# Batch 1's q and k transposed on TensorE instead of by DMA, the second weight's loads issued behind the first's, and batch 1's norms moved behind batch 0

## The chip, the cores and the metric

The kernel runs on one core of a Trainium2 chip. The metric is the device time of one execution in microseconds (us). The engines are named as in the profile: PE is TensorE's matrix multiply, PEld its weight load, DVE is VectorE, ACT ScalarE, POOL GpSimd and SP SyncE, which here only issues DMAs. The kernel's order is written by hand: an engine's instructions stand in its queue in that order, and one whose operand is not ready holds up those behind it.

## The reference

An attention with normed q and k is followed by a mixer block with a low-rank token mix:

```python
def _attn_ref(q, k, v, g_q, g_k):          # q, k, v: (8, 12, 448, 64)
    q_n, k_n = rmsnorm(q, g_q), rmsnorm(k, g_k)      # over the head's 64 values
    scores = matmul(q_n, k_n.T) / sqrt(64)
    attn = softmax(scores)
    return matmul(attn, v)

def _moe_ref(x, U, V, w_ch1, w_ch2):       # x: (8, 448, 768), heads side by side
    xt = x.transpose(0, 2, 1)
    h = xt @ U @ V                          # rank 32
    u = x + h.transpose(0, 2, 1)
    ch = maximum(u @ w_ch1, 0) @ w_ch2      # 768 -> 3072 -> 768
    return u + ch
```

Inputs and output are float32; the kernel multiplies in bf16. There are 8 batches of 448 rows, and the two weights are 9.4 MB each in float32, 4.7 MB each once they stand in SBUF as bf16.

## The kernel before

**Units.** A pair `p` is two heads of one batch; a batch has six pairs, so batch 0 has pairs 0 to 5 and batch 1 pairs 6 to 11. Loads go by triples of the form `t = p // 2`, four heads each: `load(t)` issues four 256 KB transfers on SP (q and k for the pairs 2t and 2t+1), `load_v(t)` one of 512 KB for v. Two buffers `qkL` take q and k in turn (a third lies in `hT` while that is unused), so `load(5)` needs the buffer of `load(3)`, which is read by `scale(6)` and `scale(7)`.

**The path of one pair.** `squares(p)` (POOL, L199) squares q and k; `reduce(p)` (DVE, L205) sums over 64 values into the PSUM bank `rs_bank`; `rsqrt(p, n)` (ACT, L209 and L210) takes the inverse root for n pairs at once; `scale(p)` (DVE, L218) writes normed q and k in bf16 to `qkn`. Two buffers take the squares, so `squares(p)` needs `reduce(p - 2)` done. Then q and k must be turned so that the 64 values lie on partitions (`qkT`). There are two ways:

- `transposes(p)`: eight 112x112 transposes on PE (L240) into one PSUM tile `pt`, then on DVE a multiplication of q by the gains (L242) and a copy of k (L246).
- `dma_transposes(p)`: one transposing DMA on SP (L249), SBUF to SBUF; the gains follow as `gains(p)` on ACT, in place (L254).

Batch 0 takes the first way, all later batches the second. `scores(p, kcs)` (PE, L263) then multiplies, `expo(p, kc)` (ACT, L268) exponentiates, `values(p, hh)` (PE, L284) multiplies by v, and DVE divides (L287, L288, L291). `cast_v(t)` on POOL (L188) turns v into bf16.

**The mixer.** `mix_t`, `mix_u` and `mix_x` do the low-rank mix on PE, with results taken out by DVE or ACT; `turn_u` transposes u by DMA into `uA` or `uB`. `mlp(b)` is a generator: 24 pieces of six matmuls `ph` (L364), each followed by a relu into `hT` (all on ACT for batch 0), then the second layer in pieces of six matmuls `po` (L384), `osb` on DVE (L388) and the stores on SP. PSUM tiles `ph`, `po`, `o`, `px`, `pm`, `pt` share three buffers of `ps_mm`.

**The order** is written by hand. Batch 0's attention runs first, pair by pair, in `pair(p)`. `begin` does the matmuls of the first four `ph` pieces into idle score buffers. Then, for each batch b, `weave` runs the fill `mlp(b)` between the items of `attention(b + 1)` and `mixing(b + 1)`: an item's weight sets how many columns of the fill are run before it, as a share of a total (for batch 0, 0.70 of the fill's 18,432 columns over the attention and 0.12 over the mixing; what is left runs at the end). `attention(1)` works ahead: at pair p it scales and transposes pair p + 2, and at pairs 7, 9 and 11 reduces the pairs of two triples later. It also issues `squares(10)` and `squares(11)` at pair 6, although both have been issued ahead of it.

**Weights.** `load_w1(i)` and `load_w2(half, i)` are cast during the DMA and are issued by POOL, six of each. The six of the first weight are issued within `pair(0)` to `pair(2)`, between casts and squares; those of the second stand behind all of batch 0.

Of the kernel before, what the change touches and what calls it, by code (L numbers as in the profile page):

```python
# [17 lines left out]
def kernel(  # L18
# [29 lines left out]
    NT, NP = B * 3, B * 6  # L48
# [46 lines left out]
    def rs_of(p, n=1):  # L95

        c = 16 * (p % 6)
        return rs_bank[:, c:c + 16 * n]
# [62 lines left out]
    def load_w2(half, i):  # L161
        hs, c = slice(half * HALF, (half + 1) * HALF), slice(8 * i, 8 * (i + 1))
        nc.gpsimd.dma_start(w2b[:, half, c], w2r[:, c, hs])
# [19 lines left out]
    def load_v(t):  # L183
        rows, src = heads(v, HG * t, HG)
        nc.sync.dma_start(v_of[t][0:rows], src)

    def cast_v(t):
        nc.gpsimd.tensor_copy(vas[t % NV][:, :, :, 0:D], v_of[t][0:SP].rearrange("p h (j d) -> p h j d", d=D))  # L188

    def squares(p, eng="pool", parts=(slice(0, 1024),)):  # L190
        t, a = divmod(p, 2)
        src = qk_of[t][0:SP, a].rearrange("p s h c -> p (s h c)")
        if p not in sqs:
            sqs[p] = norm.tile([SP, 2 * 2 * NJ * D], FP32, tag="sq", name="sq")
        for c in parts:
            if eng == "act":
                nc.scalar.activation(sqs[p][:, c], src[:, c], AF.Square)
            else:
                nc.gpsimd.tensor_tensor(sqs[p][:, c], src[:, c], src[:, c], OP.mult)  # L199

    def reduce(p, parts=(slice(0, 16),)):
        rs = rs_of(p)
        sq = sqs[p].rearrange("p (g d) -> p g d", d=D)
        for c in parts:
            nc.vector.tensor_reduce(rs[:, c], sq[:, c], AX, OP.add)  # L205

    def rsqrt(p, n=1):
        rs = rs_of(p, n)
        nc.scalar.activation(rs, rs, AF.Ln, bias=eps)  # L209
        nc.scalar.activation(rs, rs, AF.Exp, scale=-0.5)  # L210
# [37 lines left out]
    def dma_transposes(p):  # L248
        nc.sync.dma_start_transpose(out=qkTs[p % NQ][:, 0:SQK].rearrange("p (m r) -> p m r", r=SP),  # L249
                                    in_=qkns.pop(p).rearrange("p j g d -> p (j g d)"))  # L250

    def gains(p):
        qT = blocks(p)[:, :, 0]
        nc.scalar.activation(qT, qT, AF.Copy, scale=gg)  # L254
# [142 lines left out]
    def attention(b):  # L397
        items = []

        def add(weight, fn, *args):  # L400
            items.append((weight, lambda: fn(*args)))

        for p in range(b * 6, b * 6 + 6):
            t, odd = divmod(p, 2)
            add(1, scores, p, (0, 1))
            add(0, expo, p, 0)
            if p + 2 < NP:
                add(0, scale, p + 2)
                add(0, dma_transposes, p + 2)
            add(1, expo, p, 1)  # L410
            if p % 6:
                add(1, values, p - 1, 0)
            if t + 2 < NT:
                for a in range(2):
                    if odd:
                        add(0, reduce, 2 * t + 4 + a)
                    else:
                        add(0, squares, 2 * t + 4 + a)
            add(1, scores, p, (2, 3))
            add(0, expo, p, 2)  # L420
            if p % 6:
                add(1, values, p - 1, 1)
            if odd and t + 2 < NT:
                add(0, rsqrt, 2 * t + 4, 2)
            if odd and t + 3 < NT:
                add(0, load, t + 3)
                add(0, load_v, t + 3)
            if not odd and t + 1 < NT:
                add(0, cast_v, t + 1)
            if p + 1 < NP:  # L430
                add(0, gains, p + 1)
            add(1, expo, p, 3)
        add(1, values, b * 6 + 5, 0)
        add(1, values, b * 6 + 5, 1)
        return items

    def weave(fill, total, items):
        weights = sum(w for w, _ in items)
        done = due = 0.0
        for w, piece in items:  # L440
            due += w * total / max(weights, 1)
            while done < due:
                n = next(fill, None)
                if n is None:
                    break
                done += n
            piece()
# [22 lines left out]
    def pair(p):  # L470


        scores(p, (1,))
        expo(p, 0)
        if p == 0:
            scale(1)
        elif 1 < p < 5:
            rsqrt(p + 2)
        if 0 < p < 5:
            transposes(p + 1)  # L480
        if p >= 2:
            mix_t(0, [slice((p - 2) * P, (p - 1) * P)])
        if p:
            values(p - 1, 0)

        scores(p, (2,))
        expo(p, 1)
        if p == 0:
            transposes(1)
            reduce(2)  # L490
        elif p < 5:
            if p == 1:
                rsqrt(3)
            scale(p + 2)
        if p == 4:
            dma_transposes(6)
        if p:
            values(p - 1, 1)
        if p == 0:
            load(3)  # L500
            load_w1(0)
            cast_v(0)
            load_w1(1)
            squares(4)
            setup_late()
            load_w1(2)
        if p == 1:
            cast_v(1)
            setup_U()
            load_v(3)  # L510
            load_w1(3)
        if p == 2:
            load_w1(4)
            cast_v(2)
            load_w1(5)
            load(4)
            load_v(4)

        if 0 < p < 5:
            reduce(p + 3)  # L520
            squares(p + 5)
        scores(p, (3,))
        expo(p, 2)

        if p < 5:
            scores(p + 1, (0,))
        expo(p, 3)
        if p == 0:
            rsqrt(2)
            scale(2)  # L530
            reduce(3)
            squares(5)
        if p >= 2:
            mix_u(p - 2)

    with tc.manual_schedule():
        halves = (slice(0, 512), slice(512, 1024))
        groups = (slice(0, 8), slice(8, 16))
        load_pair(nc.sync, 0, 0, 0)
        load_pair(nc.scalar, 0, 1, 0)  # L540
        nc.scalar.preload_act_table_set("natural_log_exp_and_others")
        load_pair(nc.sync, 0, 0, 1)
        load_pair(nc.sync, 0, 1, 1)
        load_g()
        load(1)
        load_v(0)
        load_mix()
        load(2)
        load_v(1)
        load_v(2)  # L550
        setup()
        heat(NWARM)
        squares(0, "act", halves)
        squares(1, "act", halves)
        reduce(0, groups)
        rsqrt(0)
        scale(0, (slice(0, 2), slice(2, 4)))
        nc.gpsimd.tensor_mul(gg, gg, gk2)
        transposes(0)
        reduce(1)  # L560
        rsqrt(1)
        squares(2)
        squares(3)
        scores(0, (0,))
        for p in range(6):
            pair(p)
        mix_t(0, [slice(4 * P, 5 * P)])
        values(5, 0)
        mix_u(4)
        values(5, 1)  # L570
        begin(range(2), range(5))
        mix_t(0, [slice(5 * P, 6 * P)])
        begin(range(2, 4), range(5))
        mix_u(5)
        begin(range(4), (5,))
        gains(6)
        rsqrt(7)
        scale(7)
        dma_transposes(7)
        reduce(8)  # L580
        squares(10)
        cast_v(3)
        for half in range(2):
            for i in range(3):
                load_w2(half, i)
        for b in range(B):
            fill = mlp(b)
            if b == 0:
                for _ in range(4):
                    next(fill)  # L590
                load(5)
                load_v(5)
                reduce(9)
                squares(11)
                rsqrt(8, 2)
                extra = [(0, lambda i=i, h=h: mix_x(0, i, h)) for i in range(3) for h in range(2)]
                items = attention(1)
                step = len(items) // 7
                for n, x in enumerate(extra):
                    items.insert((n + 1) * step + n, x)  # L600
                weave(fill, volume(0) * 0.70, items)
                weave(fill, volume(0) * 0.12, mixing(1))
            elif b + 1 < B:
                weave(fill, volume(b % 2) * 0.72, attention(b + 1))
                weave(fill, volume(b % 2) * 0.12, mixing(b + 1))
            for _ in fill:
                pass
# [30 lines left out]
```

## Time and profile before

| | before |
|---|---|
| three runs, us | 630.65, 632.24, 633.34 (median 632.24) |
| the profiled execution's own time, us | 632.71 |
| its span, first to last instruction, us | 630.7 |
| PE busy | 592.5 us, 94% of the span |
| DVE, ACT, POOL busy | 305.7, 257.6, 130.0 us |
| mean granted TensorE clock | 0.962 of full speed |
| bytes moved by DMA | 73.63 MB |

The span's 40 slices are 15.8 us each; a digit is the busy share in tenths, and PEclk is the clock granted to TensorE:

```profile
PE   5876788999999999999999999999999999999996
POOL 6544711402023032022022033022023000000000
PEclk8668978999999999999999999999999999999999
DMA  8997999564425444464325444454425410050011
```

PE is below nine tenths in the first seven slices (110 us) and in the last. The clock is below full in the same stretch, and the 16 DMA engines are close to fully busy there; from about slice 8 on the picture repeats with a period of two batches, which is why batches 2 and 3 can serve as a measure for batches 0 and 1.

### The profile page before, as it was taken

What the parts mean: (1) busy time and instruction counts of PE and PEld (TensorE: products, weight loads), DVE (VectorE), ACT (ScalarE), POOL (GpSimd) and SP (SyncE); (2) the same over time, 40 slices, a digit from 0 to 9 for tenths busy, and PEclk for the clock granted to TensorE, in tenths of its full rate; (3) what the DMA queues carried; (4) which work ended last, traced back from release to release, by engine and by line L of the source; (5) the groups of instructions that cost most, each with busy time, mean ns of one, the idle gap of its engine ahead of it and who ended that gap; (6) DMA issues with size and microseconds to landing.
All of it is one profiled execution on the core that took longest, in us unless ns stands there. A gap on an engine that the chain in (4) does not pass through costs nothing.

```text
span 630.7 us, 11153 instructions
## 1 busy us (share of the span) xinstructions
PE 592.5 (94%) x4637; PEld 321.7 (51%) x4658; DVE 305.7 (48%) x614; ACT 257.6 (41%) x410; POOL 130.0 (21%) x111
## 2 busy tenths in 40 slices
PE   5876788999999999999999999999999999999996
PEld 2553344544455555554455555554455555554563
DVE  4853334655545366645545366645545364432211
ACT  5752564416551267316551267316551167202100
POOL 6544711402023032022022033022023000000000
PEclk8668978999999999999999999999999999999999
DMA  8997999564425444464325444454425410050011
GB/s 244 238 245 123 190 225 222 154 139 116 102 58 158 96 130 130 116 132 124 102 58 154 98 132 130 119 127 125 88 73 144 98 33 16 27 101 1 0 51 50
DMA packets 113746, 73.63 MB, mean 117 GB/s; under 512 B 62384, under 2 KB 110112, under 8 KB 113696
## 3 DMA queue, kind: packets, MB, share of 16 engines
q1 hardware_dynamic: 102160, 63.22, 40.8%
q0 software_dynamic: 10944, 9.44, 9.7%
q8 instruction: 36, 0.59, 0.4%
q10 hardware_dynamic: 592, 0.26, 0.2%
q14 instruction: 14, 0.11, 0.1%
HBM read 56.78 MB, written 11.01 MB: 107 GB/s over the span
## 4 chain that ended last, share of the span: by engine, by line
PE 75%; DMA 13%; DVE 7%; ACT 2%; issue 1%; POOL 0%; SPq 0%; DVEq 0%; ACTq 0%; POOLq 0%
PE po L384 33%; PE ph L364 29%; DMA qkT<-qkn 9%; PE sc L263 6%; PE o L284 5%; DVE rs_bank L205 4%; DMA qk<-in_k_dram 4%; PE px L334 1%; ACT E L268 1%; PE pm L313 1%; DVE hT L369 1%; ACT hT L367 1%; DMA uB<-x 1%; DVE x L288 1%; ACT qkT L254 0%
## 5 line engine op out<-in xcount | busy, mean ns | idle before, releaser
L384 PE MATMUL po<-w2b,hT 128*128 128x384 bf16 x1344 | 239.7, 328 | 1.3 <-DVE osb L388 1.3
L268 ACT ACTIVATE E<-sc 112x896 bf16<-112x896 f32 x192 | 170.4, 916 | 76.2 <-PE sc L263 75.9
L384 PEld LDWEIGHTS <-hT 128*128 128x128 bf16 x1344 | 126.7, 98 | 90.8 <-issue 13.4
L364 PEld LDWEIGHTS <-w1b 128*128 128x128 bf16 x1128 | 104.6, 99 | 118.3 <-issue 28.5
L199 POOL TENSOR_TENSOR sq<-qk 112x1024 f32<-112x1024 f32 x46 | 86.7, 1892 | 348.4 <-DMA qk<-in_k_dram 291.5
L367 ACT ACTIVATE hT<-ph 128x384 bf16<-128x384 f32 (+1 forms) x104 | 56.2, 541 | 214.8 <-PE ph L364 214.8
L364 PE MATMUL ph<-uB,w1b 128*128 128x512 bf16 x555 | 131.5, 379 | 3.1 <-DMA uB<-x 1.1
L364 PE MATMUL ph<-uA,w1b 128*128 128x384 bf16 x552 | 105.1, 337 | 5.6 <-DVE xs L291 5.2
L369 DVE TENSOR_SCALAR hT<-ph 128x512 bf16<-128x512 f32 (+1 forms) x84 | 53.2, 633 | 80.3 <-PE ph L364 80.0
L284 PEld LDWEIGHTS <-E 112*128 112x128 bf16 x1536 | 64.7, 101 | 20.3 <-DVE qkT L246 3.6
L284 PE MATMUL o<-va,E 112*128 112x65 bf16 x1536 | 69.2, 199 | 4.4 <-DVE qkT L246 3.4
L263 PE MATMUL sc<-qkT 64*128 64x448 bf16 x376 | 58.4, 373 | 11.1 <-ACT hT L367 5.3
L205 DVE TENSOR_REDUCE rs_bank<-sq 112x16 f32<-112x1024 f32 (+1 forms) x49 | 58.9, 1201 | 17.5 <-POOL sq L199 9.4
L388 DVE TENSOR_TENSOR osb<-po,x 128x384 f32<-128x384 f32 x48 | 26.8, 558 | 73.7 <-PE po L384 73.5
L218 DVE TENSOR_TENSOR qkn<-qk,rs_bank 112x1024 bf16<-112x1024 f32 (+1 forms) x47 | 55.9, 1191 | 11.0 <-ACT rs_bank L210 10.7
L287 DVE RECIPROCAL rec<-o 128x4 f32<-128x4 f32 x96 | 17.4, 181 | 88.4 <-PE o L284 88.3
L263 PEld LDWEIGHTS <-qkT 64*128 64x128 bf16 (+1 forms) x384 | 14.1, 97 | 49.7 <-issue 37.9
L288 DVE TENSOR_TENSOR x<-o,rec 128x192 bf16<-128x192 f32 x96 | 34.3, 358 | 3.3
L336 DVE TENSOR_TENSOR x<-px,x 128x384 bf16<-128x384 f32 x48 | 25.9, 554 | 18.9 <-PE px L334 18.8
L254 ACT ACTIVATE qkT<-qkT,gg 128x448 bf16<-128x448 bf16 x42 | 27.8, 662 | 9.5 <-DMA qkT<-qkn 9.5
L188 POOL CAST va<-vt 112x1024 bf16<-112x1024 f32 x23 | 23.8, 1039 | 1.7 <-DMA vt<-in_v_dram 1.7
L291 DVE TENSOR_TENSOR xs<-o,rec 64x64 bf16<-64x64 f32 x96 | 20.8, 217 | 0.7
(60 smaller groups left out, 140.4 us busy)
## 6 DMA issues: line engine op xcount, KB each, us to landing
qk<-in_q_dram SPq DMA_DIRECT2D x45, 256.0 KB, 4.3
qk<-in_k_dram SPq DMA_DIRECT2D x44, 256.0 KB, 4.6
vt<-in_v_dram SPq DMA_DIRECT2D x22, 512.0 KB, 6.0
w1b<-in_moe_w_ch_dram POOLq DMA_DIRECT2D x6, 768.0 KB, 15.1
w2b<-in_moe_w_ch_dram POOLq DMA_DIRECT2D x6, 768.0 KB, 26.8
out_dram<-osb SPq DMA_DIRECT2D x8, 336.0 KB, 2.8
out_dram<-osb SPq DMA_DIRECT2D x8, 288.0 KB, 2.8
out_dram<-osb SPq DMA_DIRECT2D x8, 240.0 KB, 2.7
```

The lines of the kernel that those rows point to most:

```text
L199: nc.gpsimd.tensor_tensor(sqs[p][:, c], src[:, c], src[:, c], OP.mult)
L205: nc.vector.tensor_reduce(rs[:, c], sq[:, c], AX, OP.add)
L218: nc.vector.tensor_tensor(qkns[p][:, :, c].rearrange("p j g d -> p g j d"), qk_of[t][0:SP, a].rearrange("p s h (j d) -> p (s h) j d", d=D) ...
L254: nc.scalar.activation(qT, qT, AF.Copy, scale=gg)
L263: nc.tensor.matmul(sc[0:n, hh, 0:S], flat[pp, c:c + n], blocks(p)[pp, :, 0], start=True, stop=True)
L268: nc.scalar.activation(Es[p % NE][:, :, PAD + kc * S:PAD + (kc + 1) * S], scs.pop((p, kc))[0:SP, :, 0:S], AF.Exp, scale=float(D) ** 0.5)
L284: nc.tensor.matmul(o[:, i, :], E[:, hh, c:c + P], va[:, hl, kc, :], start=(kc == 0), stop=(kc == NJ - 1))
L288: nc.vector.tensor_tensor(x3[:, :, d0:d0 + D], o[:, t0:t0 + 3, 0:D], rec[:, t0:t0 + 3].rearrange("p c -> p c ()").to_broadcast([P, 3, D]), ...
L364: nc.tensor.matmul(ph, w1b[:, dc, hc * P:(hc + 1) * P], u[:, dc, :], start=(dc == 0), stop=(dc == KD - 1))
L367: nc.scalar.activation(hT[:, hc, 0:n], ph, AF.Relu)
L369: nc.vector.tensor_relu(hT[:, hc, 0:n], ph)
L384: nc.tensor.matmul(po, hT[:, hc, i * P:(i + 1) * P], w2b[:, half, hc], start=(hc == 0), stop=(hc == KH - 1))
```

## The change

It has three parts. Batch 1's pairs 6 to 11 go the way of `transposes` (PE and DVE) instead of `dma_transposes` and `gains`; `attention(1)` issues `transposes(p + 1)` at pair p with weight 0.5. The six `load_w2` are issued in `pair(2)`, behind `load_w1(5)`. The norms of pairs 6 to 9 (squares, reduce, rsqrt, scale) leave `pair(1)` to `pair(4)` and stand behind batch 0 and `begin`, apart from `squares(6)` and `squares(7)`, which come in `pair(4)`. The second issue of `squares(10)` and `squares(11)` is gone. Eight pieces of the fill instead of four run ahead of `attention(1)`, and the shares of the weave go from 0.70 to 0.62 and from 0.12 to 0.08.

```diff
@@ attention(b)
             if p + 2 < NP:
                 add(0, scale, p + 2)
-                add(0, dma_transposes, p + 2)
+                if p >= 10:
+                    add(0, dma_transposes, p + 2)
...
                     if odd:
                         add(0, reduce, 2 * t + 4 + a)
-                    else:
+                    elif p > 6:
                         add(0, squares, 2 * t + 4 + a)
...
-            if p + 1 < NP:
+            if p < 11:
+                add(0.5, transposes, p + 1)
+            elif p + 1 < NP:
                 add(0, gains, p + 1)
@@ pair(p)
-        elif 1 < p < 5:
+        elif 1 < p < 4:
             rsqrt(p + 2)
...
-        elif p < 5:
+        elif p < 4:
             if p == 1:
                 rsqrt(3)
             scale(p + 2)
-        if p == 4:
-            dma_transposes(6)
...
             load_w1(5)
             load(4)
             load_v(4)
-
-        if 0 < p < 5:
+            for half in range(2):
+                for i in range(3):
+                    load_w2(half, i)
+
+        if 0 < p < 3:
             reduce(p + 3)
-            squares(p + 5)
+        if p == 4:
+            squares(6)
+            squares(7)
@@ after begin
-        gains(6)
-        rsqrt(7)
+        cast_v(3)
+        reduce(6)
+        squares(8)
+        reduce(7)
+        squares(9)
+        rsqrt(6, 2)
+        scale(6)
         scale(7)
-        dma_transposes(7)
-        reduce(8)
-        squares(10)
-        cast_v(3)
-        for half in range(2):
-            for i in range(3):
-                load_w2(half, i)
         for b in range(B):
             fill = mlp(b)
             if b == 0:
...
                 load(5)
                 load_v(5)
+                reduce(8)
+                squares(10)
                 reduce(9)
                 squares(11)
+                for _ in range(2):
+                    next(fill)
+                transposes(6)
+                for _ in range(2):
+                    next(fill)
                 rsqrt(8, 2)
...
-                weave(fill, volume(0) * 0.70, items)
-                weave(fill, volume(0) * 0.12, mixing(1))
+                weave(fill, volume(0) * 0.62, items)
+                weave(fill, volume(0) * 0.08, mixing(1))
```

## The prediction

> **What bounds the kernel now.** I read the stages first, cutting the span where the matmuls of a new batch begin (46.9 is `begin`, then mlp(1), mlp(2), ...). Columns: stage, its length, then PE, PEld, DVE, ACT, POOL busy (instructions), granted clock, DMA share, GB/s.
>
> ```profile
> 33.70:46.90 13.20, 9.82 (x111) 6.49 (x112) 7.95 (x23) 7.74 (x12) 5.95 (x5) 0.62 1.18 246
> 46.90:138.30 91.40, 74.46 (x565) 39.58 (x564) 40.55 (x78) 36.71 (x66) 32.76 (x23) 0.89 0.96 176
> 138.30:217.40 79.10, 78.52 (x594) 40.59 (x599) 38.40 (x77) 32.09 (x50) 14.26 (x9) 1.00 0.42 105
> 217.40:280.40 63.00, 62.16 (x539) 35.83 (x539) 37.23 (x76) 29.85 (x48) 14.22 (x9) 1.00 0.53 129
> 280.40:359.50 79.10, 78.53 (x594) 40.60 (x599) 39.66 (x78) 32.09 (x50) 14.26 (x9) 1.00 0.40 106
> ```
>
> From 138.3 on PE is busy all the time at full clock: it bounds, and the change touches nothing there. mlp(2) with attention(3) takes 63.0 us; the like work of mlp(0) with attention(1) takes 91.4. That stage, and the 13 us ahead of it, hold what can be had. Next the waits of PE in it (engine, line, what it waited for: us, times, longest):
>
> ```profile
> PE sc L263 <- ACT hT L367: 5.3, 2, 5.1
> PE ph L364 <- DVE xs L291: 5.2, 1, 5.2
> PE sc L263 <- ACT qkT L254: 2.4, 2, 2.2
> PE ph L364 <- DMA uB<-x: 1.1, 1, 1.1
> ```
>
> And the timeline at the three longest idle times, from 33.7 on:
>
> ```profile
> 33.23 1.88 POOL L199 TENSOR_TENSOR sq<-qk 112x1024 f32<-112x1024 f32 x1 [6.94 <-DMA qk<-in_k_dram]
> 35.15 1.23 DVE L205 TENSOR_REDUCE rs_bank<-sq 112x16 f32<-112x1024 f32 x1 [3.16 <-POOL sq L199]
> 36.28 0.44 DVE L242 TENSOR_SCALAR qkT<-pt,gg 128x448 bf16<-128x448 bf16 x1
> 37.08 1.06 PE L284 MATMUL o<-va,E 112*128 112x65 bf16 x16 [3.38 <-DVE qkT L246]
> ...
> 39.68 20.52 SPq L249 DMA_TRANSPOSE qkT<-qkn  x2
> 56.66 0.67 ACT L254 ACTIVATE qkT<-qkT,gg 128x448 bf16<-128x448 bf16 x1 [5.14 <-DMA qkT<-qkn]
> 58.49 0.56 PE L263 MATMUL sc<-qkT 64*128 64x448 bf16 x2 [5.13 <-ACT hT L367]
> ...
> 62.24 0.38 SPq L176 DMA_DIRECT2D qk<-in_q_dram  x1
> 72.11 5.59 POOL L199 TENSOR_TENSOR sq<-qk 112x1024 f32<-112x1024 f32 x3 [3.65 <-DMA qk<-in_k_dram]
> 75.89 1.23 DVE L205 TENSOR_REDUCE rs_bank<-sq 112x16 f32<-112x1024 f32 x1 [4.58 <-POOL sq L199]
> 79.87 2.10 PE L364 MATMUL ph<-uA,w1b 128*128 128x384 bf16 x6 [5.16 <-DVE xs L291]
> ```
>
> First idle time: reduce(6) stands in DVE's queue ahead of the copies of transposes(5), and waits for the squares of a load that lands at 33.2. Second: transposes(6) is a DMA issued at 39.7 into full DMA engines and lands 17 us later; ACT's gains wait for it, the relus stand behind them on ACT, and PE waits for both. Third: the two DMA transposes held SP until 60.2, so load(5) was issued at 62.2 and its squares came at 72; two of the three squares there are the second issue of pairs 10 and 11. Each of these idle times also costs clock behind it:
>
> ```profile
> 40.50:44.00 3.50, 3.50 (x43) 2.33 (x40) 2.65 (x8) 2.84 (x4) 0.10 (x1) 0.50 1.18 248
> 81.50:85.00 3.50, 2.69 (x10) 0.82 (x9) 0.03 (x1) 2.97 (x5) 0.00 (x0) 0.50 1.28 192
> 99.36 2.11 PE L384 MATMUL po<-w2b,hT 128*128 128x384 bf16 x12
> 104.98 3.79 PE L384 MATMUL po<-w2b,hT 128*128 128x384 bf16 x12
> ```
>
> The last two rows are the same work ahead of and behind the 2.2 us wait of the third row of waits: 1.7 us lost in clock.
>
> **The change part by part.** *Norms moved.* reduce(6), reduce(7) and scale(6) leave DVE's queue in batch 0, so the 3.38 us at 33.7 go. What is late next there is ACT's chain of exponentials (0.92 each):
>
> ```profile
> 43.62 0.92 ACT L268 ACTIVATE E<-sc 112x896 bf16<-112x896 f32 x1 [0.56 <-PE sc L263]
> 46.90 1.88 PE L467 MATMUL sc<-uA,w1b 128*128 128x384 bf16 x10
> 49.03 0.29 DVE L315 CAST t4b<-pm 128x128 bf16<-128x128 f32 x1 [1.21 <-PE pm L313]
> 51.75 1.89 POOL L199 TENSOR_TENSOR sq<-qk 112x1024 f32<-112x1024 f32 x1 [2.40 <-DMA qk<-in_k_dram]
> 57.69 1.22 DVE L218 TENSOR_TENSOR qkn<-qk,rs_bank 112x1024 bf16<-112x1024 f32 x1 [8.37 <-ACT rs_bank L210]
> ```
>
> The last one ends about 3.3 earlier, and the 2.4 us from there to `begin` shrink by 0.6 at full clock: `begin` at 46.9 - 3.9 = 43.0.
>
> *The way to scores(6).* PE runs begin and mix until 48.2 (24 matmuls at 0.163, which is the 12 in 2.11 us of 99.36 without the last one's tail of 0.16; 0.7 for pm and pu; 0.6 waiting for uA), two fill pieces to 50.2, transposes(6), two more to 52.7. DVE: the last t4b copy ends at 45.2 (as far behind `begin` as now), reduce(6) and reduce(7) 47.6, rsqrt 0.4, scale(6) 49.2, in time for PE; scale(7) 50.4, reduce(8) 51.6. Then comes a new wait: reduce(9) stands ahead of transposes(6)'s copies, and its squares wait for load(4), which lands at 51.75 now and, I take it, then. Squares 53.64, reduce 54.9, two copies 55.7: scores(6) at 55.8, against 58.49 now. PE idles 3.1 us: the scores need the copies, and the fill piece ahead of them needs the PSUM buffer that `pt` holds until then. The fill ahead of it is four pieces longer than now.
>
> *Transposes on PE.*
>
> ```profile
> 28.09 0.57 PE L240 MATMUL pt<-shift,qkn 112*128 112x112 bf16 x8
> 28.59 0.24 PE L313 MATMUL pm<-x,Ub 128*32 128x128 bf16 x3
> 28.70 0.45 DVE L242 TENSOR_SCALAR qkT<-pt,gg 128x448 bf16<-128x448 bf16 x1 [0.24 <-PE pt L240]
> 29.06 0.38 DVE L246 COPY qkT<-pt 128x448 bf16<-128x448 bf16 x1
> L254 ACT ACTIVATE qkT<-qkT,gg 128x448 bf16<-128x448 bf16 x42 | 27.8, 662 | 9.5 <-DMA qkT<-qkn 9.5
> ```
>
> Eight hold PE for 0.50 us (28.09 to 28.59): six pairs, 3.0 us added to the engine that bounds. DVE gets 6 x 0.83 = 5.0 us, ACT loses 6 x 0.66 = 4.0; both have room (40.6 and 36.7 of 91.4). Six DMA transposes go, and with them the waits on qkT and SP's block, so load(5) is issued when scale(6) and scale(7) are done, near 50, not at 62. Between a `transposes(p + 1)` and its scores stand two weights of fill, about 1.6 pieces or 1.6 us; the copies take 0.83 if DVE is free, and up to 2.5 more if it sits in two reduces. So each of the other five costs 0 to about 1 us; I take 0.4, nearer to the free case since reduces come only at every second pair: 2.0.
>
> The Trainium skill (TensorE: Matmul & The Clock Gate, Part 4) speaks against this part: about 275 ns for one transpose in a kernel's context. By it 48 would cost 13.2 us, not 3.0. The trace's one transpose also lasts about that long, but eight overlap in 0.57 us, so the row decides.
>
> *Second weight.* Six issues take POOL 5.3 us, from about 31 to 36; behind them squares(6) and (7) have until 45.
>
> ```profile
> 63.14 5.32 POOL L163 DMA_DIRECT2D w2b<-in_moe_w_ch_dram  x6
> q0 software_dynamic: 2712, 2.72, 72.8%
> q1 hardware_dynamic: 2714, 2.63, 44.0%
> w1b<-in_moe_w_ch_dram POOLq DMA_DIRECT2D x2, 768.0 KB, 16.5
> 36.94 0.83 POOL L159 DMA_DIRECT2D w1b<-in_moe_w_ch_dram  x1
> q0 software_dynamic: 6240, 4.72, 66.1%
> ```
>
> From 28 to 50 us (second to fourth row) the POOL queue q0 and SP's q1 move the same number of packets, although two or three weight loads are open: one queue each, turn by turn. The first weight ends near 36.94 + 16.5 = 53 either way, so a second weight behind it takes nothing from load(3) and load(4). Then its 6240 packets (last row, 60 to 110 us) at 2712 per 22 us take at most 51 us: first half by 78, all by 104. The first `po` will come near 84, the second half near 101; q1 has only three loads in that time, so it is likely earlier. load(5), from 52 at half rate, lands by 65; reduce(10) comes at pair 7, near 64. No wait of the size of the third one.
>
> *Weave.* The last turn of u now waits for a store's turn; with the mixing earlier the 1.1 us on uB go.
>
> *Sum.* From `begin` to mlp(1): 63.0 (mlp(2)'s stage) + 0.7 (last pm, pu) + 1.0 (six px of batch 0) + 3.0 (transposes) = 67.7, so 110.7 with no wait; + 0.6 (uA) + 3.1 (scores(6)) + 2.5 (clock behind it, between 1.7 as above and 3.5, half speed through two windows like 81.50:85.00) + 2.0 = 118.9. Against 138.3 that is -19.4. Everything behind keeps its length. The profiled execution took 632.71 (span 630.7, 2.0 around it): 613.3. The median of the runs stands 0.5 below it: about 613.
>
> **Rivals.** (1) *POOL blocks.* Twelve weight loads are then queued at once; the trace shows six at most. If their descriptors find no room, POOL waits to about 53, where the first weight ends, and squares(6) to (9) with a cast come one after another at 1.9: 62, reduce 63.2, scores(6) at 64, 8 later: 622. Against it: none of the twelve issues now lasts over 1.1 us. The Trainium skill (SBUF - State Buffer, "SBUF size: 192, 224, or 256?") gives 16 KiB per partition for such descriptors; no run here shows how many fit.
>
> (2) *The PSUM buffers.* `pt` holds one of three until DVE is through; if each pair costs 2 us in place of 0.4: 8 more, 621. For it: DVE's 2.5 us of reduces. Against: relus are on ACT, which loses work.
>
> (3) *Slower: load(4) late.* reduce(9) now gates scores(6). If the longer POOL queue halves SP's share from 31 on, the 2550 packets that SP still moves to 51.75 take 41 us: landing near 72, scores(6) at 76. Then 76 + 58 of remaining work (67.7 less the 9.4 done) + 4.5 as above = 139, and load(5) behind it is late for reduce(10) by about 10: near 643. It decides once load(4) lands some 19 us late, or some 10 us late with load(5) late too. Against it: equal packets with several loads open.
>
> (4) *Transposes don't overlap* at their own 0.25 us: 48 x 0.25 = 12 in place of 3: 622. The skill's sentence would be this case; the rows at 28.09 speak against it.
>
> **How the numbers follow.** Forecast 0.65 (its own range 606 to 618: every wait gone is 632.2 - 27 = 605; 1 us per transpose and full cold cost +4), POOL 0.1, PSUM 0.1, load(4) 0.08, transposes 0.03; 0.04 for parts that cancel and leave no change. The range reaches to the 620s: 606 to 624. A measurement of this kernel tells about 0.5% (3 us) from no change. Faster 0.87, same 0.05, slower 0.08.
>
> **What would show it.** Right: no idle time at 33.7; scores(6) near 56 with an idle time of about 3 us on DVE's copies, behind reduce(9); no wait of PE on qkT by ACT in the 60 to 110; mlp(1) beginning near 119; stages from there on at 79.1 and 63.0. Wrong: POOL's six issues taking over 10 us; squares(9) past 60; `po` waiting on w2b; waits on L242 and L246 adding up to over 6 us; any later stage longer.

## The result, and the profile after

The changed kernel takes 614.9 us (median of four runs, 613.01 to 615.76); the kernel before took 632.79 beside it (630.65 to 634.7). The ratio is 0.9714, with a 95% interval of 0.9675 to 0.9753. The profiled execution took 613.01 with a span of 611.2, so 19.7 us less than the profiled execution before (632.71); the forecast was 19.4 less. It was the fastest of the four: between the medians lie 17.9 us.

The same cut into stages, at `begin`, mlp(1), mlp(2), mlp(3) (columns as before: length, busy time of PE, PEld, DVE, ACT, POOL, granted clock, DMA share, GB/s):

```profile
39.40:118.50 79.10, 70.38 (x614) 39.66 (x611) 46.55 (x92) 34.15 (x61) 28.41 (x18) 0.98 1.01 211
118.50:197.60 79.10, 78.50 (x594) 40.73 (x599) 39.42 (x78) 31.67 (x48) 14.30 (x9) 1.00 0.42 106
198.00:261.00 63.00, 62.19 (x539) 35.87 (x539) 37.20 (x76) 29.88 (x48) 14.26 (x9) 1.00 0.53 129
```

The later stages still last 79.1 and 63.0 us; all of the gain lies ahead of mlp(1). `begin` comes at 39.4 instead of 46.9, and its stage lasts 79.1 instead of 91.4: 7.5 + 12.3 = 19.8. (The cut at 138.3 in the prediction stands 0.4 us behind the first matmul of mlp(1), which came at 137.9; from there to 118.5 it is 19.4.) The longest waits of PE in that stage:

```profile
PE pt L240 <- DVE qkn L218: 3.7, 1, 3.7
PE o L284 <- ACT E L268: 1.2, 1, 1.2
PE pt L240 <- DVE xs L291: 1.1, 1, 1.1
```

The waits on qkT behind DMA transposes and on uB are gone, and a wait of 3.7 us on scale(6) is new. The timeline shows where it comes from:

```profile
31.87 3.51 POOL L163 DMA_DIRECT2D w2b<-in_moe_w_ch_dram  x4
36.69 0.88 POOL L163 DMA_DIRECT2D w2b<-in_moe_w_ch_dram  x1 [1.31 <-DMA w1b<-in_moe_w_ch_dram]
42.72 0.87 POOL L163 DMA_DIRECT2D w2b<-in_moe_w_ch_dram  x1 [5.15 <-DMA w1b<-in_moe_w_ch_dram]
43.61 3.75 POOL L199 TENSOR_TENSOR sq<-qk 112x1024 f32<-112x1024 f32 x2
45.55 1.23 DVE L205 TENSOR_REDUCE rs_bank<-sq 112x16 f32<-112x1024 f32 x1 [3.80 <-POOL sq L199]
49.15 2.35 DVE L218 TENSOR_TENSOR qkn<-qk,rs_bank 112x1024 bf16<-112x1024 f32 x2 [0.53 <-ACT rs_bank L210]
50.43 0.57 PE L240 MATMUL pt<-shift,qkn 112*128 112x112 bf16 x8 [3.67 <-DVE qkn L218]
51.11 4.76 PE L364 MATMUL ph<-uA,w1b 128*128 128x384 bf16 x18
...
52.04 1.89 POOL L199 TENSOR_TENSOR sq<-qk 112x1024 f32<-112x1024 f32 x1 [1.86 <-DMA qk<-in_k_dram]
53.97 1.23 DVE L205 TENSOR_REDUCE rs_bank<-sq 112x16 f32<-112x1024 f32 x1 [1.14 <-POOL sq L199]
55.10 0.44 DVE L242 TENSOR_SCALAR qkT<-pt,gg 128x448 bf16<-128x448 bf16 x1
55.90 0.55 PE L263 MATMUL sc<-qkT 64*128 64x448 bf16 x4
```

The fifth and sixth load of the second weight wait on POOL until loads of the first have landed, so squares(6) and squares(7) come at 43.6, reduce and scale follow, and PE stands ahead of transposes(6). The second half is the forecast's: reduce(9) behind load(4), then the copies, then scores(6) at 55.9. Only the idle time ahead of them is missing. The 18 matmuls behind the wait take 4.76 us at a granted clock of 0.75 (50.0 to 56.9 us), where 12 take 2.11 at full clock, and so PE is busy until the copies are done.

### The profile page after: what moved, and what is told of

The parts are those of the page before. It is cut to its first block, busy times and chain, and to the rows that moved or that the text cites. A ratio compares the mean times of both kernels' runs of the same rounds, so it can differ in the third digit from the quotient of the medians.

```text
span 611.2 us, 11233 instructions
## 1 busy us (share of the span) xinstructions
PE 583.9 (96%) x4685; PEld 319.0 (52%) x4706; DVE 309.5 (51%) x626; ACT 254.4 (42%) x402; POOL 126.4 (21%) x109
## 3 DMA queue, kind: packets, MB, share of 16 engines
q0 software_dynamic: 10944, 9.44, 9.5%
## 4 chain that ended last, share of the span: by engine, by line
PE 81%; DVE 7%; DMA 6%; ACT 2%; issue 1%; POOL 1%; SPq 0%; DVEq 0%; ACTq 0%; POOLq 0%
PE po L384 34%; PE ph L364 33%; PE sc L263 6%; PE o L284 6%; DMA vt<-in_v_dram 6%; DVE rs_bank L205 4%; PE px L334 1%; ACT hT L367 1%; ACT E L268 1%; DMA qk<-in_k_dram 1%; DVE x L288 1%; POOL sq L199 1%; PE pm L313 1%; DVE hT L369 1%; DVE osb L388 0%
## 5 line engine op out<-in xcount | busy, mean ns | idle before, releaser
L199 POOL TENSOR_TENSOR sq<-qk 112x1024 f32<-112x1024 f32 x44 | 83.1, 1892 | 324.3 <-DMA qk<-in_k_dram 233.2
L364 PE MATMUL ph<-uA,w1b 128*128 128x384 bf16 x552 | 101.9, 330 | 1.2 <-DVE qkT L246 0.4
L284 PEld LDWEIGHTS <-E 112*128 112x128 bf16 x1536 | 62.1, 99 | 17.7 <-ACT E L268 2.6
L284 PE MATMUL o<-va,E 112*128 112x65 bf16 x1536 | 66.6, 195 | 2.6 <-ACT E L268 2.1
L388 DVE TENSOR_TENSOR osb<-po,x 128x384 f32<-128x384 f32 x48 | 26.7, 556 | 73.6 <-PE po L384 73.6
L263 PE MATMUL sc<-qkT 64*128 64x448 bf16 x376 | 55.4, 358 | 2.7 <-ACT E L268 1.6
L218 DVE TENSOR_TENSOR qkn<-qk,rs_bank 112x1024 bf16<-112x1024 f32 (+1 forms) x47 | 55.8, 1190 | 2.5 <-ACT rs_bank L210 2.2
L336 DVE TENSOR_TENSOR x<-px,x 128x384 bf16<-128x384 f32 x48 | 25.8, 552 | 12.3 <-PE px L334 12.2
L254 ACT ACTIVATE qkT<-qkT,gg 128x448 bf16<-128x448 bf16 x36 | 23.8, 660 | 0.0
```

Source lines behind the costliest of these rows:

```text
L218: nc.vector.tensor_tensor(qkns[p][:, :, c].rearrange("p j g d -> p g j d"), qk_of[t][0:SP, a].rearrange("p s h (j d) -> p (s h) j d", d=D) ...
L263: nc.tensor.matmul(sc[0:n, hh, 0:S], flat[pp, c:c + n], blocks(p)[pp, :, 0], start=True, stop=True)
L284: nc.tensor.matmul(o[:, i, :], E[:, hh, c:c + P], va[:, hl, kc, :], start=(kc == 0), stop=(kc == NJ - 1))
L364: nc.tensor.matmul(ph, w1b[:, dc, hc * P:(hc + 1) * P], u[:, dc, :], start=(dc == 0), stop=(dc == KD - 1))
L388: nc.vector.tensor_add(osb[:, hs], po, xt[i][:, hs])
```

## The experiments

Each was timed beside the kernel before. `begin`, scores(6) and mlp(1) are read in the timeline of the profiled execution, in us.

| kernel | median, us | ratio to before, 95% interval | begin | scores(6) | mlp(1) |
|---|---|---|---|---|---|
| before (first set) | 632.79 | | 46.9 | 58.5 | 137.9 |
| changed | 614.9 | 0.9714 (0.9675 to 0.9753) | 39.4 | 55.9 | 118.5 |
| e1, second weight late | 613.15 | 0.9701 (0.9685 to 0.9718) | 39.5 | 54.7 | 118.7 |
| e2, second weight early, alone | 635.96 | 1.0057 (1.0036 to 1.0077) | 52.2 | 60.4 | 139.5 |
| e3, changed, but DMA transposes | 627.59 | 0.9926 (0.991 to 0.9943) | 39.5 | 62.2 | 132.6 |
| e4, transposes doubled | 616.71 | 0.9747 (0.9722 to 0.9772) | 40.4 | 57.9 | 121.7 |
| e5, copies ahead of reduces | 610.08 | 0.9661 (0.9624 to 0.9698) | 41.2 | 51.8 | 115.6 |
| e6, second weight in two loads | 612.8 | 0.9687 (0.965 to 0.9724) | 39.5 | 54.1 | 118.8 |
| e7, norms back, PE transposes | 612.88 | 0.9693 (0.9658 to 0.9728) | 44.2 | 54.8 | 117.4 |
| e8, e5 with later reduces | 609.34 | 0.9618 (0.9594 to 0.9642) | 40.7 | 51.3 | 114.5 |
| e9, norms and fill alone | 625.21 | 0.9869 (0.9838 to 0.9901) | 41.0 | 58.9 | 132.2 |
| e10, changed again | 615.1 | 0.9712 (0.9687 to 0.9738) | 39.6 | 57.1 | 119.8 |

**e1: the second weight's loads put back.**

```diff
@@ pair(2), against the changed kernel
-            for half in range(2):
-                for i in range(3):
-                    load_w2(half, i)
@@ after begin
         squares(9)
+        for half in range(2):
+            for i in range(3):
+                load_w2(half, i)
         rsqrt(6, 2)
```

> The changed kernel with the second weight's six issues put back behind batch 0, behind squares(9). Theory A (the early issue brings nothing by itself): the second weight's packets start when the first weight's end, near 53 us, in both; POOL no longer waits ahead of squares(6), so transposes(6) comes some 2 us earlier and its 3.7 us of idle PE shrink, but the scores of pair 6 stay near 56, held by reduce(9) and load(4). Time 613 to 617 us. Rival (the early issue carries part of the gain): PE waits for the second weight at the first po, 620 us or more.

613.15 us: as theory A has it. POOL does squares(6) at once and issues the second weight at 52.6, behind squares(9); the last load of the first weight, issued at 29.4, landed 26.7 us later. transposes(6) comes 3.8 us earlier, and the idle time of PE moves from there to the scores and grows from 3.7 to 4.5 us. Rows of e1's timeline:

```profile
32.87 1.89 POOL L199 TENSOR_TENSOR sq<-qk 112x1024 f32<-112x1024 f32 x1 [2.65 <-DMA qk<-in_k_dram]
52.64 5.32 POOL L163 DMA_DIRECT2D w2b<-in_moe_w_ch_dram  x6
54.66 0.55 PE L263 MATMUL sc<-qkT 64*128 64x448 bf16 x4 [4.53 <-DVE qkT L246]
```

No `po` waits for the weight here either. The early issue adds nothing to the gain that the times show: the intervals of e1 and of the changed kernel overlap.

**e2: that part alone, on the kernel before.** The six `load_w2` go from behind batch 0 to behind `load(4)` and `load_v(4)` in `pair(2)`, as in the change.

> The kernel before with only the second weight's issues moved behind load_w1(5). Theory A: alone this part is a loss. The fifth and sixth issue wait on POOL for first-weight loads to land, near 43 us, so squares(7) comes near 44 instead of 38.7, reduce(7) holds DVE and with it batch 0 about 5 us longer, and the two DMA transposes run beside weight packets from 53 on: 636 to 642 us. Rival (earlier weights are a gain by themselves): 625 to 630 us.

635.96 us, 0.57% slower (0.36 to 0.77%), just under what was expected. Rows of POOL, DVE and PE in its timeline:

```profile
44.08 0.88 POOL L163 DMA_DIRECT2D w2b<-in_moe_w_ch_dram  x1 [4.76 <-DMA w1b<-in_moe_w_ch_dram]
44.97 5.60 POOL L199 TENSOR_TENSOR sq<-qk 112x1024 f32<-112x1024 f32 x3
46.91 1.23 DVE L205 TENSOR_REDUCE rs_bank<-sq 112x16 f32<-112x1024 f32 x1 [9.91 <-POOL sq L199]
48.38 0.50 PE L321 MATMUL pu<-V,t4b 128*128 128x384 bf16 x1 [8.88 <-DVE t4b L315]
```

Only the sixth issue is held. It keeps squares(7) back, reduce(7) keeps DVE, and PE idles 8.9 us within batch 0. Most of it is made good later: in the profiles `begin` is 5.3 late, scores(6) 1.9 and mlp(1) 1.6, since pair 6 was going to wait for its DMA transposes anyway.

**e3: DMA transposes back, all else as changed.**

```diff
-                if p >= 10:
-                    add(0, dma_transposes, p + 2)
+                add(0, dma_transposes, p + 2)
...
-            if p < 11:
-                add(0.5, transposes, p + 1)
-            elif p + 1 < NP:
+            if p + 1 < NP:
                 add(0, gains, p + 1)
@@ after begin: dma_transposes(6) behind scale(6), dma_transposes(7) behind scale(7); gains(6) for transposes(6)
```

> The changed kernel with batch 1's q and k transposed by DMA again, all else as changed. Theory A (the transposes on PE carry more than half of the gain): the two first DMA transposes go turn by turn with weight packets, about 7 us each from 53 on, so scores(6) come near 61 to 65, SP is held and load(5) lands near 78, reduce(10) late by about 8: 622 to 632 us. Rival (the norms moved out of batch 0 carry it, and DMA transposes would be hidden by the longer fill): 612 to 617 us.

627.59 us: theory A. The transposes of pairs 6 and 7 were issued at 52.1, the first landed near 61, load(5) was late for its squares until 70 (78 was expected), and two waits on qkT came to 11.0 us. The next two transposes (fourth row) held SP for 14.1 us:

```profile
52.14 4.61 SPq L249 DMA_TRANSPOSE qkT<-qkn  x2
61.49 0.67 ACT L254 ACTIVATE qkT<-qkT,gg 128x448 bf16<-128x448 bf16 x1 [8.35 <-DMA qkT<-qkn]
62.22 0.93 PE L263 MATMUL sc<-qkT 64*128 64x448 bf16 x4 [5.76 <-ACT qkT L254]
64.60 14.10 SPq L249 DMA_TRANSPOSE qkT<-qkn  x2
PE sc L263 <- ACT qkT L254: 11.0, 2, 5.8
```

**e9: the norms and the longer fill alone** is e3 with the second weight's issues behind squares(9), as in e1.

> The kernel of e3 (batch 1 transposed by DMA) with the second weight's issues behind squares(9): the norms moved and the longer fill alone. Theory A (the DMA transposes are what holds pair 6 and SP, whatever stands around them): scores(6) near 57 to 60, load(5) issued only behind both transposes, 621 to 628 us. Rival (norms and transposes carry like shares of the gain): 617 us or less.

625.21 us: theory A. `begin` is at 41.0, 6 us earlier than before the change, and mlp(1) comes 5.7 earlier. The stage between them keeps its length (91.2 us, 91.0 before), since three waits on qkT take 16.0 us in it:

```profile
58.85 0.93 PE L263 MATMUL sc<-qkT 64*128 64x448 bf16 x4 [7.58 <-ACT qkT L254]
PE sc L263 <- ACT qkT L254: 16.0, 3, 7.6
```

**e7: the norms back in batch 0, transposes on PE** (e1 with `pair(1)` to `pair(4)` issuing reduce, squares, rsqrt and scale as in the kernel before).

> The kernel of e1 with the norms of pairs 6 to 9 back in batch 0, as in the kernel before, but batch 1 still transposed on PE. Theory A (load(4) holds scores(6) to about 55 in any case, so the 3.4 us in batch 0 and the idle time ahead of scores(6) are largely the same time): the idle 3.4 us near 33 comes back, the 4.5 us ahead of scores(6) go, 613 to 617 us. Rival (each idle time counts by itself, with its clock): 618 to 622 us.

612.88 us, just under theory A's 613 to 617: the idle time does not count twice. reduce(6) holds batch 0 again, though PE stands idle there for 1.6 us and not for 3.4. `begin` is 4.7 later than in e1, of which 1 to 2 us are the clock of the first 30 us (see the end), and scores(6) come at the same time. Rows of DVE, PE and POOL, and its stage from `begin` to mlp(1):

```profile
33.30 1.23 DVE L205 TENSOR_REDUCE rs_bank<-sq 112x16 f32<-112x1024 f32 x1 [1.43 <-POOL sq L199]
35.23 0.68 PE L284 MATMUL o<-va,E 112*128 112x65 bf16 x16 [1.59 <-DVE qkT L246]
48.61 1.90 POOL L199 TENSOR_TENSOR sq<-qk 112x1024 f32<-112x1024 f32 x1 [2.42 <-DMA qk<-in_k_dram]
54.79 0.55 PE L263 MATMUL sc<-qkT 64*128 64x448 bf16 x4
44.19:117.42 73.23, 68.31 (x613) 39.13 (x610) 43.01 (x89) 34.13 (x61) 29.12 (x21) 1.00 1.01 208
```

There is no wait ahead of scores(6) now: load(4) has landed at 48.6, the copies end at 53.6, and PE comes to the scores at 54.8 with its own work. Whether PE stands idle in batch 0 or ahead of pair 6, it comes to the same.

**e4: each of batch 1's transposes done twice.** `for s in range(2)` becomes `for s in [0, 1] * (2 if p > 5 else 1)`.

> The changed kernel with each of batch 1's 48 transposes done twice on PE, into the same place. Theory A (PE bounds the stage and eight transposes hold it 0.50 us): six times 0.50 = 3.0 us more, 617 to 619 us. Rival B (PE has 8.7 us of idle time in the stage that takes them up): within 1 us of 615. Rival C (a transpose holds PE for its own 0.21 to 0.28 us): 10 to 13 us more, 625 to 628.

616.71 us, just under theory A's 617 to 619, against 614.9 and 615.1 of the changed kernel: its ratio lies 0.0033 to 0.0035 higher, some 2 us, but the intervals overlap. The profiles are clearer. The first row is the changed kernel's, the others are e4's:

```profile
59.22 0.57 PE L240 MATMUL pt<-shift,qkn 112*128 112x112 bf16 x8
61.20 0.96 PE L240 MATMUL pt<-shift,qkn 112*128 112x112 bf16 x16
40.42:121.70 81.28, 73.10 (x662) 42.61 (x659) 46.74 (x92) 34.07 (x61) 28.43 (x18) 0.96 1.00 202
```

At full clock eight transposes hold PE for 0.40 us (the next matmul starts at 59.62) and sixteen for 0.80 (it starts at 62.00). PE is busy 2.7 us longer in e4's stage than in the changed kernel's (73.1 against 70.4, and 70.5 in e10). The stage is 2.2 longer than in the first profile of the changed kernel and 1.2 longer than in e10 (80.1). So one set costs PE 2.7 us, and the stage some 1 to 2. Rival C (10 us and more) falls; rival B (within 1 us) is not shut out by the times, but both profiles speak against it.

**e6: the second weight in two loads** instead of six, in the changed kernel's place (`load_w2` takes 24 pieces of a half at once).

> The changed kernel with the second weight in two loads of one half each instead of six, at the same place: as many bytes and packets, eight weight loads in all instead of twelve. Theory A (POOL waits because at most eight weight loads may be open): no wait on POOL at these issues, squares(6) near 34 instead of 43.6, transposes(6) 2 us earlier, time as e1, 612 to 615 us. Rival (there is no room for more packets): POOL waits for the first weight at the second of the two, to near 40, as now.

612.8 us: theory A. There are about as many packets (10,880 on POOL's queue in the whole execution, against 10,944) in eight weight loads, and POOL doesn't wait:

```profile
29.58 2.83 POOL L163 DMA_DIRECT2D w2b<-in_moe_w_ch_dram  x2
32.41 1.93 POOL L199 TENSOR_TENSOR sq<-qk 112x1024 f32<-112x1024 f32 x1
54.06 0.93 PE L263 MATMUL sc<-qkT 64*128 64x448 bf16 x4 [3.84 <-DVE qkT L246]
```

So what held POOL was the number of open loads (in the changed kernel the eleventh waits for the third to land, and the twelfth for the fourth: eight open), not room for packets. Whether the chip sets this number or the program that is built from the kernel, no run shows. Scores(6) and the time are as in e1, since reduce(9) holds them anyway.

**e5: the copies ahead of the reduces**, on e1.

```diff
                 for _ in range(2):
                     next(fill)
                 transposes(6)
+                reduce(8)
+                squares(10)
+                reduce(9)
+                squares(11)
                 for _ in range(2):
                     next(fill)
-                rsqrt(8, 2)
@@ these four stood ahead of the first two next(fill); attention(1): scale(8) not at the head of pair 6
             add(1, expo, p, 3)
+            if p == 6:
+                add(0, rsqrt, 8, 2)
+                add(0, scale, 8)
```

> The kernel of e1 with transposes(6) ahead of reduce(8) and reduce(9) in DVE's queue; rsqrt(8, 2) and scale(8) go to the end of pair 6 so that ACT and DVE aren't held there. Theory A (what holds pair 6's scores is only the place of reduce(9), which waits for load(4), ahead of the copies): scores(6) near 50 instead of 54.7, the idle 4.5 us of PE and the slow clock behind it go, 606 to 609 us. Rival (load(4) gates the stage anyway, by scale(8) and the copies of pair 7): the idle time comes back at pair 7, 612 to 614 us.

610.08 us, between the two; its interval and e1's just overlap. The wait ahead of pair 6 is gone, and the clock stays full through the whole stage (1.00, third value from the end of the last row):

```profile
49.36 0.38 DVE L246 COPY qkT<-pt 128x448 bf16<-128x448 bf16 x1
51.81 0.55 PE L263 MATMUL sc<-qkT 64*128 64x448 bf16 x4
52.45 1.23 DVE L205 TENSOR_REDUCE rs_bank<-sq 112x16 f32<-112x1024 f32 x1 [1.57 <-POOL sq L199]
65.53 2.11 PE L364 MATMUL ph<-uA,w1b 128*128 128x384 bf16 x12 [1.61 <-DVE xs L291]
41.21:115.62 74.41, 68.56 (x614) 39.41 (x612) 46.48 (x92) 34.09 (x61) 29.16 (x21) 1.00 1.04 217
```

The stage is 4.8 us shorter than e1's (79.23), so theory A's mechanism stands. The fourth row shows 1.6 us of a new wait, in pair 7, where the rival had looked for it. The first 30 us also ran slower in this profile (see the end). Together the two are of the size of what is missing to 606 to 609; for the clock this is an argument and not a test.

**e8: reduce(10), reduce(11) and their rsqrt behind the copies of pair 8**, at the end of pair 7, on e5.

> The kernel of e5 with reduce(10), reduce(11) and their rsqrt at the end of pair 7, behind the copies of transposes(8). Theory A (the 1.6 us that PE idles at 65.5 in e5 is the PSUM buffer of pt, held while DVE does the two reduces): that wait goes, about 608.5 us. Rival (DVE's two reduces then hold scale(10) and the copies of pair 8 in the same way): as e5, 609.5 to 611.

609.34 us (0.9618, 0.9594 to 0.9642), between the two expectations. The 1.6 us wait is gone, as theory A has it; three smaller ones of 0.16, 0.2 and 0.55 us stand in its place, and the stage is 0.65 shorter than e5's. Beside e10, the changed kernel again (0.9712, 0.9687 to 0.9738), this is the fastest version, clear of both kernels; e5 and e8 can't be told apart by their intervals.

> The changed kernel once more, beside the two that follow. Every theory: 613 to 615 us. In its profile's first 30 us the clock may come to full near 20 us or up to 7 us later, as it did in the profiles so far; if the begin of the first ph matmuls moves with it (39.4 us with an early clock, 41 with a late one), that part of the shift of begin is not the change's.

e10's 615.1 us agree with the first measurement. Its clock is early (0.84 from 20.6 to 24.0 us) and `begin` comes at 39.6, yet scores(6) and mlp(1) come 1.2 us later than in the first profile: POOL's last issue was held until 44.0 instead of 42.7, and PE waited 4.7 us ahead of transposes(6).

## Why the prediction was right, point by point

- **The sum** (-19.4 forecast; -19.7 measured between the profiled executions, -17.9 between the medians) and mlp(1) at 118.9 (118.5, and 119.8 in e10) came out, with two of its terms off in opposite ways. That it came within 0.3 us is luck, since two profiles of the changed kernel lie 1.2 apart. That the two errors cancel is more than luck: the forecast took the time of scores(6) from load(4) and not from `begin`.
- **`begin`, forecast 43.0, came at 39.4.** This is the term that was mis-sized: 7.5 us earlier, not 3.9. I let the last exponential end 3.3 us earlier; it ended 6.5 earlier, at 38.1 instead of 44.5:

```profile
34.74 3.34 ACT L268 ACTIVATE E<-sc 112x896 bf16<-112x896 f32 x4
39.41 1.79 PE L470 MATMUL sc<-uA,w1b 128*128 128x384 bf16 x10
```

Four exponentials run without a gap. I had kept ACT's gaps of the trace before, which came from PE at half clock, and some 1.2 us of the shift were there ahead of 33 us: the clock, below. Where the clock of the changed batch 0 is as late as in the trace before (e4, e5, e8, e9), `begin` comes at 40.4 to 41.2, so about 6 of the 7.5 us are the edit's.
- **The stage, forecast 75.9, took 79.1.** From `begin` to scores(6) it took 16.5 us in place of 12.8, and from there to mlp(1) 62.6 in place of 63.1. What the earlier `begin` won, PE lost again ahead of scores(6), which came where they were forecast (55.9 and 55.8). In e1 and e6, where nothing holds POOL, it is the same: PE waits 4.5 and 3.8 us for the copies behind load(4), and the stage takes 79.2.
- **POOL.** The step that failed is that squares(6) and squares(7) "have until 45" behind POOL's issues and scale(6) comes "in time for PE". Rival 1 came in part: POOL was held to 43.6, not to 53, and by a count of open loads, not by room (e6). The six issues took 11.7 us from first to last, over the 10 that were named as a sign of being wrong. PE waited 3.7 us ahead of transposes(6) instead of 3.1 ahead of the scores. This cost little, at most some 2 us: in the two profiles of the changed kernel scores(6) come 1.2 and 2.4 later than in e1, mlp(1) 0.2 earlier and 1.1 later, and the ratios of e1 and e6 lie 0.001 to 0.003 lower, within the intervals.
- **Which part carries the gain** I had not asked for, and the sum hides it. The transposes on PE, with the longer fill, give all of it by themselves (e7: 0.9693); the norms and the fill alone give 1.3% (e9: 0.9869); with the transposes the norms add nothing (e1: 0.9701), in this order of DVE's queue; in e5's order it was not tried. The longer fill and the dropped second issue of squares(10) and squares(11) stand in e7 and in e9 alike, and what they give by themselves was not tried either. The early second weight loses 0.6% alone (e2) and adds nothing beside the others (e1).
- **Transposes at 3.0 us of PE**: the six sets held PE for 2.7 us, 0.40 each at full clock and 0.68 for the first, and a second set made it busy 2.7 us longer (e4). The row of eight in 0.57 us was the right one, and rival 4 (0.25 us for each, 12 in all) fell. By the 275 ns for one that the Trainium skill gives (TensorE: Matmul & The Clock Gate, Part 4), an estimate for a second set is 13 us; the trace does not agree.
- **The queues.** Between 28 and 50 us, after the change:

```profile
q0 software_dynamic: 2712, 2.72, 72.7%
q1 hardware_dynamic: 2713, 2.63, 44.0%
50.44 0.37 SPq L176 DMA_DIRECT2D qk<-in_q_dram  x1
```

Turn by turn as before, so rival 3 (load(4) late) fell: squares(9) began at 52.04, against 51.75. The last load of the first weight landed at 55.1 (31.05 + 24.0), 2 us later than the forecast's 53, and no `po` waited for a weight. load(5) was issued at 50.4, as forecast.
- **The other five transposes**: waits of 0.4, 0.35 and 1.1 us, 1.9 in all, against 2.0 forecast. Rival 2 fell. The wait on uB went, as forecast. Not forecast were waits of 1.2 us on an exponential (0.3 before) and of 0.5 us on DVE in the mixing.
- **A slip**: in the trace before the last t4b copy ends 2.4 us behind `begin` (49.32), not 2.2. Nothing hangs on it.

## What to carry to other kernels

When several idle times stand ahead of one late transfer, ask what the last of them waits for: here load(4) set pair 6, and idle time taken out ahead of it came back behind it until the copies were moved ahead of the reduce that waits for that load (e5). A transposing DMA that shares busy DMA engines, and holds its queue and a second engine behind it, can be dearer than 3 us on the engine that bounds (here some 13 us, e3 against the changed kernel). Issuing a load earlier gains nothing where its queue is full until the same moment, and what stands behind the issue pays for it (e1, e2).

## What the runs showed of the hardware

The clock of the first 30 us is not the same from run to run, for nearly the same work. Granted clock (third value from the end) from 20.6 to 24.0 us before the change, after it, and in e4, whose batch 0 is that of the changed kernel:

```profile
20.60:24.00 3.40, 2.77 (x27) 1.40 (x24) 2.50 (x7) 2.72 (x5) 2.12 (x2) 0.50 1.18 250
20.60:24.00 3.40, 2.58 (x41) 1.51 (x37) 3.09 (x10) 2.75 (x5) 2.66 (x2) 0.94 1.18 250
20.60:24.00 3.40, 2.77 (x28) 1.40 (x25) 2.50 (x7) 2.68 (x5) 3.31 (x5) 0.50 1.16 245
```

The changed kernel, e1, e3, e6 and e10 show 0.82 to 0.94 there and begin at 39.4 to 39.6; e4, e5, e8 and e9 show 0.50 and, with the same batch 0, begin at 40.4 to 41.2. So 1 to 2 us of a single profile's time are this clock and not the edit, and a forecast read from one profile carries that error. The Trainium skill (TensorE: Matmul & The Clock Gate, Part 1) says that the gate watches a free-running window of about 3.4 us that does not start with the kernel; this agrees with a clock that differs between runs of like work, but it was not tried by itself.
